# Gated hidden values made transposed, with gates spread over rows by way of DRAM

## The chip, the cores and the metric

One core of a Trainium2 chip. The metric is the device time of one execution in microseconds. In the profile PE is TensorE, DVE is VectorE, ACT is ScalarE, POOL is GpSimd, and SP is the engine that issues most DMAs.

## What is computed

Spatially reduced attention, and then a mixture of eight rank-16 adapters of which each token uses two. In the reference's terms, cut to what matters (B = 4, C = 128, 12288 queries and 768 keys for each b, N = 49152 tokens in all, E = 8, r = 16):

```python
kv_pool = kv.reshape(B, H // 4, 4, W // 4, 4, C).mean(axis=(2, 4))
k = v = kv_pool.reshape(B, -1, C) @ w_sr
a = softmax(q @ k.T / sqrt(C))
x = (a @ v).reshape(N, C)
logits = x @ w_gate                      # (N, 8)
top2 = the two largest logits;  w = softmax over these two
out = x + sum over e in top2 of w[e] * ((x @ A[e]) @ B[e])
```

With all A side by side (128 x 128, columns (e, r)) and all B stacked (rows (e, r)), the last line is `x + ((x @ A) * gate) @ B`, where a token's gate of e stands for 16 columns and is zero for six of the eight experts. Of two logits the softmax is (1 + tanh(d / 2)) / 2; the half is put into B.

## The kernel before

The tokens are worked in 96 chunks of 512 (24 for each b), each of four subtiles of 128. A chunk passes through these steps; each helper writes instructions in the order in which its engine will run them, since the schedule is by hand and every engine runs its own list in order.

- `scores(c, r)`, three times a chunk: two 512-column matmuls (L284) of two key tiles with the chunk's transposed queries `qT` into `sg` (two buffers of two PSUM banks), and one exponential of 1024 columns on ACT (L285) into `tt`.
- `weigh(c, h)`, twice a chunk: 12 matmuls of 137 columns (L297), weights `tt`, moving `vext` (values, values times gate matrix, ones), into `xps`.
- `normalise(c)`: on DVE a reciprocal (L304), the product `xn` (L308; output values and logits) and four MAX8 (L315).
- `gate(p)` and `gate_weights(p)` for a pair p of chunks: small operations on POOL (L324 to L327, L334, L335) with a tanh on ACT (L332) between; result `gw`, tokens in rows.
- `transposed(cx, ch)`: PE transposes the upper half of `xn` of chunk cx and the gated hidden `hg` of chunk ch, four matmuls of 128 columns each (L352), into one bank `t_ps`; its `evacuate` copies both to `xh` in one DVE operation (L361).
- `down(c)`: four matmuls with x transposed as weights and A moving (L375), into `h_ps`, tokens in rows; `apply_gate(c)`: DVE multiplies by the gates (L380) into `hg`.
- `up(c)`: four matmuls with hg transposed as weights and B moving (L400), into `d_ps`; `give(c)`: DVE adds `xn` (L407) into `osb`, and SP stores 256 KB (L413).

In iteration c of the main loop (c = 2 to 94) PE's list is: scores; the first half of weigh(c-1); scores; up(c-6); the second half of weigh(c-1); transposed(c-2, c-4); scores; down(c-3). `h_ps` and `d_ps` share one PSUM bank (`mtile`), `t_ps` is one bank, `xps` two, `sg` four: all eight. In odd iterations `gate_weights` of the pair c-3, c-2 is issued after the first scores.

Queries: `cast_q(g)` (POOL's DMA) writes 2048 rows as float16 to DRAM, `load_q(g)` (L274, SP) transposes all 2048 by one DMA into one of three buffers. Keys and values of the next b are loaded by SP (L85, 512 KB each, the last issued in iteration 55), summed on POOL and projected in the loop's `prep_step`. The first two query groups are `q0`, in a buffer of the kv pool, and `q1`, in one of its own.

After the loop come the run-out (weighing of chunks 94 and 95, and the steps of the last chunks, written out singly) and a range check that decides about a slow exact path, which isn't taken here.

Of the kernel before, what the change touches and what calls it, by code (L numbers as in the profile page):

```python
# [21 lines left out]
def kernel(  # L22
# [36 lines left out]
    ps_x = ctx.enter_context(tc.tile_pool(name="ps_x", bufs=1, space=bass.MemoryType.PSUM))  # L59
    ps_t = ctx.enter_context(tc.tile_pool(name="ps_t", bufs=1, space=bass.MemoryType.PSUM))  # L60
    ps_h = ctx.enter_context(tc.tile_pool(name="ps_h", bufs=1, space=bass.MemoryType.PSUM))
    score_banks = ExitStack()
# [8 lines left out]
    q_h = qdram.tile([B * N, C], F16)  # L71
    qflat = q.rearrange("b n c -> (b n) c")
# [8 lines left out]
    def load_row(b, t, d):  # L81
        if d == 0:
            kvt[b, t] = kvpool.tile([P, 4, 2, 4 * C], FP32, tag="kvt", name="kvt")
        src = kv[b].rearrange("(t h d) (w e) c -> t d h w (e c)", t=NT, d=4, e=8)
        nc.sync.dma_start(kvt[b, t][:, d].rearrange("p u c -> p (u c)"), src[t, d])  # L85
# [11 lines left out]
    q1 = kvpool.tile([P, GROWS // NTOK, NS, C], FP32, tag="q1", name="q1", bufs=1)  # L97
    q0 = kvpool.tile([P, GROWS // NTOK, NS, C], FP32, tag="kvt", name="q0")
# [37 lines left out]

    rinv_all = keep.tile([P, NCH, NS], FP32, name="rinv_all")
    vss = keep.tile([P, 2 * B], FP32, name="vss")
    kpT, kfT, vext, sqsum = {}, {}, {}, {}
    for b in range(B):  # L140
        kpT[b] = keep.tile([P, NKV], FP32, name=f"kpT{b}")
# [130 lines left out]
    def load_q(g):  # L272
        qT[g] = qpool.tile([P, GROWS], F16, tag="qT", name="qT")
        nc.sync.dma_start(qT[g], q_h[g * GROWS:(g + 1) * GROWS], transpose=True)  # L274
# [55 lines left out]
    def gate_weights(p, eng):  # L330
        th = small.tile([P, 2 * NS, E], FP32, tag="th", name="th")
        nc.scalar.activation(th, garg[p], AF.Tanh, bias=0.0, scale=0.5)  # L332
        gw[p] = small.tile([P, 2 * NS, E], FP32, tag="gw", name="gw")
# [3 lines left out]
    def transposed(cx, ch, bank=None):  # L337

        if bank is None:
            t_ps = ps_t.tile([P, 2, NS, P], BF16, tag="tp", name="t_ps")  # L340
        else:
            t_ps = bank.bitcast(BF16).rearrange("p (k s c) -> p k s c", k=2, s=NS)
# [6 lines left out]
        if not todo:  # L349
            return lambda act=False: None  # L350
        for i, (k, s, src) in enumerate(todo):
            mm(t_ps[:, k, s], src, id_bf, is_transpose=True,  # L352
               start=(i == 0), stop=(i == len(todo) - 1), skip_group_check=True)

        def evacuate(act=False):
            xh = run.tile([P, 2, NS, P], BF16, tag="xh", name="xh", bufs=5)
            lo, hi_ = todo[0][0], todo[-1][0] + 1
            if act:
                nc.scalar.activation(xh[:, lo:hi_], t_ps[:, lo:hi_], AF.Copy)  # L359
            else:  # L360
                nc.vector.tensor_copy(xh[:, lo:hi_], t_ps[:, lo:hi_])  # L361
            if lo == 0:
                xT[cx] = xh[:, 0]
            if hi_ == 2:
                hgT[ch] = xh[:, 1]

        return evacuate
# [35 lines left out]
    def give(c, how="add", queue=None):  # L403

        osb = run.tile([P, NS, P], FP32, tag="osb", name="osb", bufs=8)
        if how == "add":
            nc.vector.tensor_tensor(osb, dps[c], xn[c][:, :, 0:C], op=ALU.add)  # L407
        else:
            nc.scalar.activation(osb, dps[c], AF.Copy)
        if how == "pool":  # L410
            nc.gpsimd.tensor_tensor(osb, osb, xn[c][:, :, 0:C], op=ALU.add)  # L411
        t0 = c * NTOK
        (queue or nc.sync).dma_start(  # L413
            out[t0:t0 + NTOK, :].rearrange("(p s) c -> p s c", p=P), osb)

    def chunk_ok(c):
        return 0 <= c < NCH
# [121 lines left out]
    load_q(2)  # L539
# [10 lines left out]
    NQ = NCH // GRP  # L550
    for c in range(2, NCH - 1):
        b, k = divmod(c, CPB)
        cs = c + 2
        if cs < NCH and cs % GRP == 0:
            g = cs // GRP
            if g + 2 < NQ:
                load_q(g + 2)
            if g + 3 < NQ:
                cast_q(g + 3)
# [231 lines left out]
```

## Time and profile before

| | us |
|---|---|
| median of 3 runs (394.89 to 395.4) | 394.91 |
| the profiled execution | 395.21 |
| its span, first to last instruction | 393.4 |
| PE / DVE / ACT / POOL busy | 377.9 / 323.4 / 305.9 / 206.9 |
| mean granted TensorE clock | 0.997 |

A row of a timeline has start, duration, engine, line, operation, tiles and shapes, the number of merged instructions, and in brackets the idle time before it with what ended it. A row of a group has busy time and the mean ns of one behind the bar, then the idle time before. "To landing" is from a DMA's issue to its completion. Matmuls overlap, so a matmul's duration is longer than the distance to the next one's start.

### The profile page before, as it was taken

How to read it: one execution, taken by the hardware profiler on the slowest of the kernel's cores; microseconds unless marked ns; L12 is line 12 of the kernel's file. 1: busy time of each engine (PE TensorE's matmuls, PEld its weight loads, DVE VectorE, ACT ScalarE, POOL GpSimd, SP SyncE). 2: the span in 40 equal slices, each digit the busy share in tenths (PEclk: the TensorE clock that was granted, in tenths of full speed). 3: DMA queues.
4: the chain of work that ended last, by engine and by line, in shares of the span. 5: the costliest groups of instructions: out<-in, count | busy, mean ns of one | idle time of the engine just before them, and what ended most of it. 6: DMA issues, size and time to landing. Idle time of an engine off the chain costs nothing.

```text
span 393.4 us, 11525 instructions
## 1 busy us (share of the span) xinstructions
PE 377.9 (96%) x4589; PEld 301.2 (77%) x4589; DVE 323.4 (82%) x911; ACT 305.9 (78%) x387; POOL 206.9 (53%) x389
## 2 busy tenths in 40 slices
PE   4989999999999999999999999999999999999993
PEld 1457768888887887888878888888788888878882
DVE  3776777888888889888888888888888888888984
ACT  1558888878888888887877888888878877877863
POOL 1011598895688666563487666573442332322353
PEclk9999999999999999999999999999999999999998
DMA  8989997998898899298997998275678583222124
GB/s 255 393 279 167 358 262 229 275 218 218 258 211 234 256 164 266 83 211 246 238 238 225 241 237 211 92 166 130 135 92 205 136 188 102 88 82 83 55 86 160
DMA packets 69784, 76.47 MB, mean 194 GB/s; under 512 B 49664, under 2 KB 49920, under 8 KB 69376
## 3 DMA queue, kind: packets, MB, share of 16 engines
q1 hardware_dynamic: 67264, 63.45, 55.8%
q0 software_dynamic: 704, 11.54, 16.9%
q10 hardware_dynamic: 1760, 0.73, 0.7%
q8 instruction: 36, 0.59, 0.6%
q14 instruction: 20, 0.16, 0.1%
HBM read 50.53 MB, written 36.70 MB: 222 GB/s over the span
## 4 chain that ended last, share of the span: by engine, by line
PE 93%; ACT 2%; DMA 1%; POOL 1%; DVE 1%; issue 0%; ACTq 0%; POOLq 0%
PE xps L297 34%; PE sg L284 31%; PE t_ps L352 11%; PE d_ps L400 5%; PE h_ps L375 5%; PE w_ps L495 2%; PE v_ps L173 1%; DMA w_gate_sb<-in_moe_w_gate_dram 1%; ACT tt L285 1%; PE k_ps L198 1%; PE kp_ps L165 1%; ACT qT L481 0%; PE t_ps L477 0%; ACT xh L359 0%; POOL osb L411 0%
## 5 line engine op out<-in xcount | busy, mean ns | idle before, releaser
L285 ACT ACTIVATE tt<-sg 128x1024 f16<-128x1024 f32 x288 | 281.3, 1024 | 57.2 <-PE sg L284 56.8
L284 PE MATMUL sg<-qT,kfT 128*128 128x512 f16 x576 | 171.0, 379 | 1.3 <-ACT tt L285 1.0
L297 PEld LDWEIGHTS <-tt 128*128 128x128 f16 x2304 | 152.6, 112 | 22.1 <-DVE xn L308 0.7
L297 PE MATMUL xps<-vext,tt 128*128 128x137 f16 x2304 | 169.4, 223 | 0.0
L407 DVE TENSOR_TENSOR osb<-d_ps,xn 128x512 f32<-128x512 f32 x90 | 62.3, 692 | 35.3 <-PE d_ps L400 35.2
L324 POOL TENSOR_TENSOR arg<-xn,top 128x64 f32<-128x64 f32 x47 | 14.9, 317 | 121.6 <-DVE top L315 116.5
L308 DVE TENSOR_TENSOR xn<-xps,rinv_all 128x548 f32<-128x548 f32 x96 | 70.0, 729 | 3.3
L380 DVE TENSOR_TENSOR hg<-h_ps,gw 128x512 bf16<-128x512 f32 x93 | 63.2, 679 | 2.4 <-PE h_ps L375 2.4
L149 POOL TENSOR_TENSOR kvt<-kvt 128x1024 f32<-128x1024 f32 x27 | 63.9, 2368 | 1.3 <-PE sg L284 1.1
L361 DVE COPY xh<-t_ps 128x1024 bf16<-128x1024 bf16 (+1 forms) x93 | 62.5, 672 | 0.0
L284 PEld LDWEIGHTS <-kfT 128*128 128x128 f16 x576 | 45.0, 98 | 3.6 <-issue 2.1
L375 PEld LDWEIGHTS <-xh 128*128 128x128 bf16 x384 | 29.3, 98 | 21.5
L400 PEld LDWEIGHTS <-xh 128*128 128x128 bf16 x384 | 29.1, 98 | 21.5 <-ACT xh L359 0.6
L315 DVE MAX8 top<-xn 128x8 f32<-128x8 f32 x384 | 35.9, 156 | 3.3
L352 PE MATMUL t_ps<-id_bf,hg 128*128 128x128 bf16 x376 | 36.3, 219 | 0.5 <-ACT xh L359 0.5
L352 PE MATMUL t_ps<-id_bf,xn 128*128 128x128 bf16 x376 | 36.3, 219 | 0.0
L400 PE MATMUL d_ps<-b_bf,xh 128*128 128x128 bf16 x368 | 35.6, 219 | 0.5 <-ACT xh L359 0.5
L375 PE MATMUL h_ps<-a_bf,xh 128*128 128x128 bf16 x372 | 35.9, 219 | 0.0
L352 PEld LDWEIGHTS <-xn 128*128 128x128 bf16 x384 | 26.4, 98 | 0.7 <-DVE xn L308 0.4
L352 PEld LDWEIGHTS <-hg 128*128 128x128 bf16 x384 | 25.3, 98 | 0.9 <-DVE hg L380 0.8
L334 POOL TENSOR_SCALAR th<-th 128x64 f32<-128x64 f32 x48 | 18.0, 375 | 13.7 <-ACT th L332 13.5
L304 DVE RECIPROCAL rinv_all<-xps 128x4 f32<-128x4 f32 x96 | 17.5, 183 | 7.5 <-PE xps L297 5.0
(112 smaller groups left out, 240.2 us busy)
## 6 DMA issues: line engine op xcount, KB each, us to landing
kvt<-in_kv_dram SPq DMA_DIRECT2D x48, 512.0 KB, 6.1
out_dram<-osb SPq DMA_DIRECT2D x94, 256.0 KB, 3.0
q_h<-in_q_dram POOLq DMA_DIRECT2D x22, 512.0 KB, 7.1
q<-in_q_dram SPq DMA_DIRECT2D x2, 1024.0 KB, 9.9
out_dram<-osb ACTq DMA_DIRECT2D x2, 256.0 KB, 3.5
qT<-q_h SPq DMA_TRANSPOSE x22, 8.4
w_in<-in_w_sr_dram ACTq DMA_DIRECT2D x1, 64.0 KB, 1.8
a_f<-in_moe_A_dram ACTq DMA_DIRECT2D x1, 64.0 KB, 10.5
```

Of the source, the lines that this page charges most:

```text
L149: eng.tensor_tensor(v[:, 0], v[:, 0], v[:, d], op=ALU.add)
L284: mm(sg[:, k], kfT[b][:, j * P:(j + 1) * P], qc, start=True, stop=True)
L285: nc.scalar.activation(tt[c][:, 2 * r:2 * r + 2], sg, AF.Exp, bias=0.0, scale=scale)
L297: mm(o, tt[c][:, j, rows], vext[b][:, j, 0:VW], start=(j == 0 and s % 2 == 0), stop=(j == NJ - 1 and s % 2 == 1), skip_group_check=True)
L308: nc.vector.tensor_tensor(xn[c].rearrange("p (b s) v -> p b s v", b=2), xv, ri.rearrange("p (b s) -> p b s", b=2).unsqueeze(3).broadcast_t ...
L315: nc.vector.max(gin[c // 2][:, (c % 2) * NS + s], xn[c][:, s, C:C + E])
L352: mm(t_ps[:, k, s], src, id_bf, is_transpose=True, start=(i == 0), stop=(i == len(todo) - 1), skip_group_check=True)
L361: nc.vector.tensor_copy(xh[:, lo:hi_], t_ps[:, lo:hi_])
L375: mm(hps[c][:, s], xT[c][:, s], a_bf, start=(s == 0), stop=(s == NS - 1))
L380: nc.vector.tensor_tensor(hg[c].rearrange("p s (e r) -> p (s e) r", r=RK), hps[c].rearrange("p s (e r) -> p (s e) r", r=RK), g.rearrange(" ...
L400: mm(dps[c][:, s], hgT[c][:, s], b_bf, start=(s == 0 and fresh), stop=(s == NS - 1), skip_group_check=True)
L407: nc.vector.tensor_tensor(osb, dps[c], xn[c][:, :, 0:C], op=ALU.add)
```

## The change

For chunks 28 to 89 (`FAR`) the hidden values are made with rows (e, r) and tokens in columns: A is the weight and x transposed moves, one matmul of 512 columns. What `up` needs comes out of the multiplication directly, and hg is not transposed. The gates must then lie in the same layout, each in 16 rows: PE transposes the gates of a pair of chunks (128 columns, into the free part of `t_ps`), DVE copies 64 rows of it to `g_sb`, SP stores these to DRAM (`g_h`, 16 KB), and SP loads them back with each row repeated 16 times (`ge`, 256 KB a pair).

```diff
+    def load_gates(p):
+        gE[p] = run.tile([P, 2 * NS, P], F16, tag="ge", name="ge", bufs=3)
+        nc.sync.dma_start(
+            gE[p].rearrange("p s t -> p (s t)"),
+            g_h[p].rearrange("e s t -> e (s t)").unsqueeze(1).broadcast_to([E, RK, 2 * NS * P]))
+
+    def gated_hidden(c):
+        h_ps = mtile([P, NS, P], name="h_ps")
+        mm(h_ps, a_bf, xT[c], start=True, stop=True)
+        hgT[c] = run.tile([P, NS, P], BF16, tag="ht", name="ht", bufs=3)
+        nc.vector.tensor_tensor(hgT[c], h_ps, gE[c // 2][:, (c % 2) * NS:(c % 2 + 1) * NS],
+                                op=ALU.mult)
...
+        def later():                         # in transposed(cx, ch, p)
+            if p < NCH:
+                k = p % 4 // 2 * 2
+                mm(t_ps[:, 1, 0].bitcast(F16),
+                   gw_all[:, k:k + 2].rearrange("p k s e -> p (k s e)"), id_h,
+                   is_transpose=True, start=False, stop=True, skip_group_check=True)
...
+            if p < NCH:                      # in its evacuate
+                g_sb = small.tile([P, P], F16, tag="gt", name="g_sb", bufs=2)
+                copy(g_sb[rows], t_ps[rows, 1, 0].bitcast(F16))
+                nc.sync.dma_start(g_h[p].rearrange("e s t -> s e t"), g_sb[rows])
...
+    FAR = range(28, NCH - 6)
+    for x in FAR[::2]:
+        late = x == FAR[0]
+        sent[x + 3 + late] = x // 2
+        fetched[x + 4 + late] = x // 2
+    for x in range(NCH - 6):
+        far = x in FAR
+        made.setdefault(x + (6 if far else 3), []).append(x)
+        ups.setdefault(x + (7 if far else 6), []).append(x)
+        if not far:
+            turns[x + 4] = x
     for c in range(2, NCH - 1):
...
-        if chunk_ok(c - 6):
-            up(c - 6)
-            give(c - 6)
+        for x in ups.get(c, ()):
+            up(x)
+            give(x)
+        if c in fetched:
+            load_gates(fetched[c])
         weigh(c - 1, 1)
...
-        evacuate = transposed(c - 2, c - 4)
+        later, evacuate = transposed(
+            c - 2, turns.get(c, c - 4 if c == NCH - 2 else NCH),
+            sent.get(c, NCH))
         next_scores()
+        g, i = divmod(c + 2 * GRP, GRP)
+        if g < NQ:
+            load_q(g, i)
         prep(c)
...
-        if chunk_ok(c - 3):
-            down(c - 3)
-            apply_gate(c - 3)
+        for x in made.get(c, ()):
+            if x in FAR:
+                gated_hidden(x)
+            else:
+                down(x)
+                apply_gate(x)
+        later()
...
         evacuate(c == NCH - 2)
```

So a far chunk x (x even) has its pair's gates transposed in iteration x+3, fetched in x+4, and is multiplied in x+6 and x+7; `up` comes one iteration later than before. For other chunks the order is as before.

Besides: `load_q(g, k)` transposes 512 rows at a time, for chunk c+8 in iteration c. q0 and q1 share one kv buffer. The last kv tile is loaded in halves. The pooled keys stand in one tile. `osb` has six buffers instead of eight. The store of osb is split from its making (`take`, `add`, `add_rows`, `put`).

The run-out has a new order. The gates of chunks 94 and 95 are made chunk by chunk (94 on POOL, 95 on DVE), with MAX8 into the same places; chunk 95's weighing has banks of its own. Its list, with the loop's last steps, is in short:

```python
weigh(94, 0); gated_hidden(89); up(88); give(88); weigh(94, 1); tops4(94)
transposed(93, 91) -> ACT; up(89); h2 = hidden(92); up(90); gate_args(94) on POOL
weigh(95, 0); gated(92); turn x of 94; h3 = hidden(93); gated(93); weigh(95, 1)
up(91); tanh of 94; gate_w(94) on POOL; tops4(95); turn hg of 92; hidden(94); turn hg of 93
x_first(93); turn x of 95; gate_args(95), tanh of 95; up(92); gated(94); up(93); gate_w(95)
hidden(95); gated(95); POOL adds x of 89 to 92 to what ACT copied from d; puts
turn hg of 94; turn hg of 95 in two halves (ACT, DVE); up(94); give(94)
up(95) in two halves: ACT copies one (x added by PE), DVE adds x to the other; put(95)
```

`turn` is four transposes and a copy (ACT), `hidden` is `down` without the gate, `gated` is the multiplication of `apply_gate`.

299 lines of the change are left out of this document (204 added, 95 removed).

## The prediction

> **What bounds the kernel now.** I read the page first: the busy shares, then the chain that ended last.
>
> ```profile
> PE 377.9 (96%) x4589; PEld 301.2 (77%) x4589; DVE 323.4 (82%) x911; ACT 305.9 (78%) x387; POOL 206.9 (53%) x389
> ```
>
> ```profile
> PE 93%; ACT 2%; DMA 1%; POOL 1%; DVE 1%; issue 0%; ACTq 0%; POOLq 0%
> ```
>
> TensorE (PE) is busy 96% of the span, and 93% of the chain is its own work. A busy PE is not proof, so I went on to the timeline of one steady iteration, PE's rows and then VectorE's (DVE's): the starts of successive groups give the rate.
>
> ```profile
> 202.18 0.59 PE L284 MATMUL sg<-qT,kfT 128*128 128x512 f16 x2
> 202.61 0.39 PE L400 MATMUL d_ps<-b_bf,xh 128*128 128x128 bf16 x4
> 202.83 0.88 PE L297 MATMUL xps<-vext,tt 128*128 128x137 f16 x12
> 203.55 0.39 PE L352 MATMUL t_ps<-id_bf,xn 128*128 128x128 bf16 x4
> 203.77 0.39 PE L352 MATMUL t_ps<-id_bf,hg 128*128 128x128 bf16 x4
> 204.00 0.59 PE L284 MATMUL sg<-qT,kfT 128*128 128x512 f16 x2
> 204.43 0.39 PE L375 MATMUL h_ps<-a_bf,xh 128*128 128x128 bf16 x4
> 204.65 0.59 PE L284 MATMUL sg<-qT,kfT 128*128 128x512 f16 x2
> 205.08 0.88 PE L297 MATMUL xps<-vext,tt 128*128 128x137 f16 x12
> 205.80 0.59 PE L284 MATMUL sg<-qT,kfT 128*128 128x512 f16 x2
> 206.24 0.39 PE L400 MATMUL d_ps<-b_bf,xh 128*128 128x128 bf16 x4
> ```
>
> ```profile
> 203.03 0.69 DVE L407 TENSOR_TENSOR osb<-d_ps,xn 128x512 f32<-128x512 f32 x1 [0.37 <-PE d_ps L400]
> 203.75 0.18 DVE L304 RECIPROCAL rinv_all<-xps 128x4 f32<-128x4 f32 x1
> 203.97 0.73 DVE L308 TENSOR_TENSOR xn<-xps,rinv_all 128x548 f32<-128x548 f32 x1
> 204.73 0.37 DVE L315 MAX8 top<-xn 128x8 f32<-128x8 f32 x4
> 205.03 0.67 DVE L380 TENSOR_TENSOR hg<-h_ps,gw 128x512 bf16<-128x512 f32 x1
> 205.61 0.68 DVE L361 COPY xh<-t_ps 128x1024 bf16<-128x1024 bf16 x1
> ```
>
> From d_ps to the next d_ps is 206.24 - 202.61 = 3.63 us, the time of a chunk. No PE row has an idle note, and the starts follow at the length of the work: two 512-column score matmuls 0.43 (204.00 to 204.43), four 128-column ones 0.22 (203.55 to 203.77). So PE sets the loop by throughput, and work taken from PE comes off the time one for one until the next engine or chain is reached.
>
> **PE in the loop.** For 62 chunks (28 to 89) the change takes away four transposes of hg (L352) and four matmuls of h (L375), and puts in one 512-column matmul of h, plus one 128-column transpose of gates per pair of chunks. Removed: 248 transposes at 0.45/8 = 0.056 us (203.55 to 204.00 for eight) is 13.9, and 248 h matmuls at 0.22/4 = 0.055 is 13.6. Added: 62 x 0.43/2 = 13.3, and 31 x 0.056 = 1.7. The net is 12.5 us, or 0.20 a chunk: 3.63 becomes 3.43. Everything else on PE keeps its count.
>
> **DVE.** It keeps osb, reciprocal, xn, the maxima and one gating multiply of 512 elements; I take the multiply at its present 0.67, as only its second operand changes. The copy of xh halves, and once per pair a copy of 64 rows of 128 gates comes in.
>
> ```profile
> L361 DVE COPY xh<-t_ps 128x1024 bf16<-128x1024 bf16 x90 | 61.3, 681 | 0.0
> ```
>
> ```profile
> L361 DVE COPY xh<-t_ps 128x512 bf16<-128x512 bf16 x3 | 1.2, 415 | 0.0
> ```
>
> So 0.27 goes; the gate copy, by the slope of these two rows (0.266 per 512 elements), is 0.415 - 0.2 = 0.22, on alternate chunks. DVE now works from 203.03 to 206.29, 3.26 us of 3.63. It will need 3.0 and 3.2 of 3.43. Two of its chains run back into PE. First, d_ps to the gating multiply's end is 205.70 - 202.61 = 3.09, and the next d_ps (same bank) starts a period later: 0.54 to spare now, 0.34 after. Second, xn ends at 204.70 and the next weighing overwrites its bank at 205.08: 0.38 now. PE has 0.22 less between weighing and weighing (the hg transposes), and the h matmul is as long as the four were, so 0.16 is left, 0.05 more where a gate transpose stands. Both still fit, the second narrowly.
>
> **ScalarE (ACT).**
>
> ```profile
> 202.83 0.26 ACT L332 ACTIVATE th<-arg 128x64 f32<-128x64 f32 x1
> 202.97 1.03 ACT L285 ACTIVATE tt<-sg 128x1024 f16<-128x1024 f32 x1
> 204.63 2.89 ACT L285 ACTIVATE tt<-sg 128x1024 f16<-128x1024 f32 x3 [0.63 <-PE sg L284]
> ```
>
> Three exponentials start (2.89 - 1.02)/2 = 0.93 apart when they run together, so 2.8 a chunk plus half a tanh (0.26/2). Far from 3.43. The distance from the third scores of a chunk to the second of the next, within which an exponential must free the bank, is unchanged, since h takes as long as before.
>
> **The gates' way.**
>
> ```profile
> 203.63 0.32 POOL L335 TENSOR_TENSOR gw<-th,msk 128x64 f32<-128x64 f32 x1
> ```
>
> The gates are done on POOL at 203.95 in their iteration; PE transposes them after h, at about 204.4 on the shortened scale, so PE does not wait while POOL is on time; its long kv sums stand behind these weights in program order. DVE's copy follows the multiply and ends at about 205.95 on this scale; SP then stores 16 KB. One iteration on, SP waits for the store to land and issues a 256 KB load that repeats each row 16 times; the gating multiply needs it three iterations after 205.03, at 205.03 + 3 x 3.43 = 215.3. So store, wait and load together have 215.3 - 206.0 = 9.3 us. Chunk 28 alone is sent an iteration late and has 5.9. What do transfers take? The nearest rows are the puts of osb, 256 KB each, first for 160 to 185 us (kv loads running), then for 250 to 300 (none left):
>
> ```profile
> DMA to landing us min/median/max: 2.0/4.1/8.6
> ```
>
> ```profile
> DMA to landing us min/median/max: 2.0/2.2/8.2
> ```
>
> The two trips are 2 x 4.1 = 8.2 in the first case, and 2 x 2.2 = 4.4 in the second; the ends are 2 x 2.0 = 4.0 and 2 x 8.6 = 17.2. I take the medians: hidden in both, by 1.1 and by 4.9. Behind SP's wait stand the next query transpose, used six iterations later, and the next put, whose osb is ready about a period later; nobody waits for either. The osb buffers fall from eight to six, some 20 us, against puts that land in 8.6 at most: zero.
>
> **Is there room in the DMA engines?**
>
> ```profile
> 190.00:210.00 20.00, 20.00 (x254) 16.08 (x253) 17.48 (x52) 16.41 (x19) 12.27 (x22) 1.00 0.98 264
> 310.00:330.00 20.00, 20.00 (x259) 16.30 (x257) 17.62 (x51) 16.44 (x20) 6.45 (x19) 1.00 0.49 121
> 350.00:370.00 20.00, 20.00 (x258) 16.26 (x256) 18.24 (x52) 16.35 (x20) 5.41 (x16) 1.00 0.18 68
> ```
>
> ```profile
> kvt<-in_kv_dram SPq DMA_DIRECT2D x48, 512.0 KB, 6.1
> out_dram<-osb SPq DMA_DIRECT2D x94, 256.0 KB, 3.0
> ```
>
> In the three windows the last columns are DMA share and GB/s. At 350 to 370 there are only puts: 0.18 x 20 / (20/3.63) = 0.65 us of all engines each. A gate load moves as much to SBUF, so it adds some 0.65 per 6.9 us, a tenth of the engines. That is nothing at 310, and it fills the engines at 190 to 210, where the share is 0.98 already; the kv loads end with chunk 55, so 10 of the 31 pairs are stored beside them. The Trainium skill ("DMA: Bandwidth & Descriptors", the sections on why a DMA increments its semaphore by 16 and Rules for kernel authors) speaks against the load's shape: a pattern whose slowest dimension is 8, as here, runs on 8 of the 16 engines, so these would carry twice that share; by it I estimate a fifth instead of a tenth on half the engines, and up to 4 us of the gain gone in the kv stretch, so 387 for 383. No row of before shows a load of that shape. It raises the chance of the first rival below and not the sum.
>
> **Queries by chunk.** Each 512 KB transpose becomes four, at the same bytes, each issued six iterations ahead. The wait of SP for a free qT falls away, as the buffer asked for has been read out by then:
>
> ```profile
> SPq L274 <- PE sg L284: 38.7, 9, 6.6
> ```
>
> SP's idle time is worth nothing itself; I take zero. A quarter transpose has six iterations, 6 x 3.43 = 20.6 us, to land. The smaller edits (q0 and q1 in one kv buffer, one tile for the pooled keys, the last kv tile in halves) touch loads that lie iterations ahead: zero, covered by that lead; if the second kv batch came late behind q1 it would cost at most about one load, 6 us, which is inside the first rival's price.
>
> **The run-out.** Rows of its two ends, and of two kinds of step in it:
>
> ```profile
> 379.84 1.60 PE L297 MATMUL xps<-vext,tt 128*128 128x137 f16 x24
> ```
>
> ```profile
> 387.79 0.69 DVE L407 TENSOR_TENSOR osb<-d_ps,xn 128x512 f32<-128x512 f32 x1 [0.17 <-PE d_ps L400]
> ```
>
> ```profile
> L409 ACT ACTIVATE osb<-d_ps 128x512 f32<-128x512 f32 x2 | 1.2, 597 | 0.6 <-PE d_ps L400 0.6
> ```
>
> ```profile
> L324 DVE TENSOR_TENSOR arg<-xn,top 128x64 f32<-128x64 f32 x1 | 0.2, 236 | 0.0
> ```
>
> Weighing ends at 381.44, the last DVE operation at 388.48: 7.0 us, then 4.9 to the span's end at 393.4 (the span as the page gives it) for the last put. In the new order the last chunk goes reciprocal, xn, maxima (1.3), gate arguments (four like L324, 0.9), tanh, weight, multiply (0.26 + 0.24 + 0.67 = 1.2), a half transpose, a half copy (0.3), up, and an add of 256 (0.4): with some 0.2 for each of four hand-overs (the 0.37 ahead of osb holds one) about 5 us of dependent steps if each engine is free. But ACT has five earlier copies of 0.6 (L409 above) queued from about 381.4 on ahead of that tanh, so I place tanh's end 3.4 after the weighing, not 2.5, and two more copies of 0.6 ahead of the last chunk's; the last add then ends at about 6.7. That gains 0.3; the bounds are 2.0 (only the dependent steps) and -1.5 (two and a half more copies in the way). After 381.44 the old order has 56 matmuls of 128 columns in bfloat16, the new one 48; so 8 x 0.056 = 0.4 of the 12.5 lies where PE waits for others, and is not gained.
>
> **Sum.** The profiled execution took 395.21 us, 1.8 beside its span of 393.4. 395.2 - 12.5 + 0.4 - 0.3 = 382.8. The median of the runs is 394.91, 0.3 less, within what runs differ by; I say 383. About 0.2%, 0.8 us, is what a measurement can tell.
>
> **Rivals.**
>
> *The gate loads come late beside the kv loads.* For it: share 0.98, puts up to 8.6, so a pair can need more than 9.3. Against it: quarter transposes leave shorter queues ahead of a store. If the ten pairs lose 0.4 to 1.0 us each, 4 to 10 are lost: 387 to 393. The rule on 8 engines above is one way into this case.
>
> *Slower than before: the round trip sets the pace.* Where store and load take L, three chunks pass in L + 1.0 (206.0 - 205.03) or more, so the chunk takes (L + 1.0)/3: at L = 9.9 this is 3.63 and the whole gain is gone, at L = 10.5 it is 3.83 and 62 x 0.2 = 12 us are lost against before, 407. It decides when the mean trip exceeds 9.9. For it: SP holds all transfers behind its wait, and two medians in the loaded stretch already make 8.2. Against it: after 250 us they make 4.4, so this must hold in a stretch with free engines too.
>
> *DVE takes over.* If xn, at 0.16 to spare, holds the weighing by another 0.1 a chunk, 62 x 0.1 = 6 are lost: 389. For it: the margin; against it: DVE itself has 0.2 idle per chunk.
>
> *PE does not speed up.* If the one 512-column h matmul exposes its weight load and drain, or PE waits for the gates' transpose, 0.2 a chunk is given back: no change, 395. The score matmuls of the same width run at 0.215 with nothing exposed, which speaks against it.
>
> **Numbers.** Forecast as summed, 380 to 387: 0.62. First rival, 387 to 393: 0.18. DVE, 387 to 391: 0.07. No change: 0.03. Slower: 0.10. The range 380 to 392 leaves out the last two, a little of the first rival, and a better run-out below 380. Faster: 0.62 + 0.18 + 0.07 = 0.87.
>
> **What would show it.** Right: a d_ps-to-d_ps period near 3.43 from chunk 34 on, no idle note ahead of PE rows in the loop; the multiply on the gate tile never waits for a DMA; the last weighing ends about 12 us earlier, and the last DVE operation some 6.7 after it. Wrong: a wait list led by the multiply for its gate load, or by the weighing for xn; a period that differs between the kv stretch and after; SP waits for gate stores of 5 us and more.

## The result and the profile after

The changed kernel is slower: 439.18 us (median of 4 runs, 436.22 to 445.06) against 395.15 of the kernel before in the same session, a ratio of 1.108 (95% interval 1.100 to 1.116). 383 was predicted, with a range up to 392. Medians and ranges are of all runs; some executions of any kernel here fall into a state that makes them some per cent longer, and the ratios leave these out, so that e13, with one run left, has none, and e14's and e18's are lower than their medians would give. The profiled execution took 436.22 us, its span is 434.4, the mean granted clock 0.96.

The page of the changed kernel, busy shares and chain:

```profile
PE 379.4 (87%) x4190; PEld 286.2 (66%) x4190; DVE 316.6 (73%) x943; ACT 308.8 (71%) x391; POOL 206.2 (47%) x393
```

```profile
PE 59%; DMA 28%; DVE 7%; ACT 2%; SPq 2%; issue 1%; POOL 0%; DVEq 0%; ACTq 0%
```

PE was on 93% of the chain and is on 59%; DMA had 1% and has 28%, some 120 us. Which DMA, and who waits for it, the list of waits says (total, times, longest):

```profile
PEld L443 <- DVE ht L409: 48.7, 23, 10.5
DVE ht L409 <- DMA ge<-g_h: 44.5, 16, 10.5
PE d_ps L443 <- DVE ht L409: 37.9, 14, 10.0
...
PEld L310 <- DVE xn L321: 10.0, 45, 0.4
```

The gating multiply (L409) waits for the load of the gates 16 times, and `up` (L443) waits for the multiply: the first of the signs of being wrong that the prediction named. The last row is the narrow chain from `xn` to the weighing: often late, never by more than 0.4 us.

The second sign, a period that differs between the kv stretch and after, came too (table below); the third, SP waiting 5 us and more for a gate store, did not. SP's own list of waits from 149 to 273 us, while the kv loads run, is led by

```profile
SPq L400 <- DMA g_h<-g_sb: 25.3, 11, 3.2
```

that is 25.3 us in 11 waits, none over 3.2; over the whole run it is 44.4.

Where no load is waited for, the loop is as forecast. PE's and DVE's timelines of the changed kernel:

```profile
205.80 0.39 PE L443 MATMUL d_ps<-b_bf,ht 128*128 128x128 bf16 x4
...
207.40 0.38 PE L407 MATMUL h_ps<-xh,a_bf 128*128 128x512 bf16 x1
207.61 0.22 PE L369 MATMUL t_ps<-id_h,gw_all 128*128 128x128 f16 x1
...
209.25 0.39 PE L443 MATMUL d_ps<-b_bf,ht 128*128 128x128 bf16 x4
```

```profile
188.79 0.23 DVE L378 COPY g_sb<-t_ps 64x128 f16<-64x128 f16 x1
...
204.82 0.67 DVE L409 TENSOR_TENSOR ht<-h_ps,ge 128x512 bf16<-128x512 f32 x1
205.41 0.41 DVE L378 COPY xh<-t_ps 128x512 bf16<-128x512 bf16 x1
```

From d_ps to d_ps is 3.45 us. Now the path of one pair's gates. The chain in order of time (start, us, what), and SP's own list over the same stretch:

```profile
174.80 4.00 DMA g_h<-g_sb
...
178.87 5.88 DMA ge<-g_h
...
187.29 5.45 DMA g_h<-g_sb
...
192.76 3.56 DMA ge<-g_h
```

```profile
187.29 0.62 SPq L383 DMA_DIRECT2D g_h<-g_sb  x1
187.95 3.15 SPq L462 DMA_DIRECT2D out_dram<-osb  x1
192.76 0.60 SPq L400 DMA_DIRECT2D ge<-g_h  x1
193.47 1.15 SPq L287 DMA_TRANSPOSE qT<-q_h  x1
194.72 0.52 SPq L462 DMA_DIRECT2D out_dram<-osb  x1
195.29 1.16 SPq L287 DMA_TRANSPOSE qT<-q_h  x1
196.50 0.59 SPq L93 DMA_DIRECT2D kvt<-in_kv_dram  x1
197.19 0.62 SPq L383 DMA_DIRECT2D g_h<-g_sb  x1
```

Two delays add up. Store and load take 9.9 and 9.0 us, not 8.2. And the store starts late: the copy that ended at 189.02 is stored at 197.19, because SP was held 3.15 us in the issue of a put, then waited 1.7 at the load for the store before it (under way for 5.45 in all), and then had 4.4 us of issuing to do, two transposes of 1.15 among it. SP goes round in 9.9 us for two chunks, which should take 6.9. From 149 to 273 us its issues add up to 87.5 us and its waits for gate stores to 25.3, of 124: the list is nearly full.

Over the 14 pairs of chunks 28 to 55 the medians are 5.6 us from the copy's end to the issue of its store (longest 15.8), 3.7 from there to the issue of the load, and 5.8 from there to the multiply where that waited. Over the 17 pairs of chunks 56 to 89 they are 1.8, 2.0 and 5.3. From the copy's end to the first multiply by its gates a pair takes 15.1 us on average in the first group and 10.8 in the second; 9.3 was foreseen.

Where each kernel loses is read from the start of the reciprocal of a chunk in DVE's timeline. The table has the time from one chunk's to another's, for these two kernels and five of the experiments:

| chunks (us) | before | changed | e1 | e11 | e16 | e17 | e18 |
|---|---|---|---|---|---|---|---|
| 28 to 56 | 104.8 | 136.8 | 100.0 | 110.2 | 104.8 | 104.8 | 104.8 |
| 56 to 90 | 125.1 | 130.7 | 118.9 | 121.3 | 124.5 | 125.1 | 119.5 |
| 93 to the end | 16.8 | 19.6 | 19.5 | 23.7 | 19.5 | 18.9 | 18.3 |

Against e1, in which store and load are left out, the changed kernel loses 36.8 us in chunks 28 to 56, beside the kv loads, and 11.8 in chunks 56 to 90.

### The profile page after: what moved, and what is told of

The parts are those of the page before. It is cut to its first block, busy times and chain, and to the rows that moved or that the text cites. A ratio compares the mean times of both kernels' runs of the same rounds, so it can differ in the third digit from the quotient of the medians.

```text
span 434.4 us, 11005 instructions
## 1 busy us (share of the span) xinstructions
PE 379.4 (87%) x4190; PEld 286.2 (66%) x4190; DVE 316.6 (73%) x943; ACT 308.8 (71%) x391; POOL 206.2 (47%) x393
## 4 chain that ended last, share of the span: by engine, by line
PE 59%; DMA 28%; DVE 7%; ACT 2%; SPq 2%; issue 1%; POOL 0%; DVEq 0%; ACTq 0%
PE xps L310 23%; PE sg L297 19%; DMA ge<-g_h 16%; DMA g_h<-g_sb 10%; PE t_ps L361 5%; PE d_ps L443 4%; DVE ht L409 2%; DMA kvt<-in_kv_dram 2%; PE h_ps L407 2%; PE h_ps L418 1%; DVE xn L321 1%; ACT tt L298 1%; PE v_ps L183 1%; PE w_ps L547 1%; SPq L287 1%
## 5 line engine op out<-in xcount | busy, mean ns | idle before, releaser
L297 PE MATMUL sg<-qT,kfT 128*128 128x512 f16 x576 | 173.8, 385 | 1.4 <-ACT tt L298 1.0
L310 PEld LDWEIGHTS <-tt 128*128 128x128 f16 x2304 | 155.5, 113 | 23.8 <-DVE xn L321 10.0
L409 DVE TENSOR_TENSOR ht<-h_ps,ge 128x512 bf16<-128x512 f32 x62 | 42.2, 680 | 45.6 <-DMA ge<-g_h 44.5
L443 PE MATMUL d_ps<-b_bf,ht 128*128 128x128 bf16 x240 | 24.3, 226 | 38.2 <-DVE ht L409 37.9
L443 PEld LDWEIGHTS <-ht 128*128 128x128 bf16 x248 | 17.6, 100 | 58.1 <-DVE ht L409 48.7
L378 DVE COPY xh<-t_ps 128x512 bf16<-128x512 bf16 (+1 forms) x92 | 45.6, 495 | 0.5
L407 PE MATMUL h_ps<-xh,a_bf 128*128 128x512 bf16 x62 | 24.5, 395 | 0.1
L423 DVE TENSOR_TENSOR hg<-h_ps,gw_all 128x512 bf16<-128x512 f32 x30 | 20.4, 680 | 1.0 <-PE h_ps L418 1.0
L340 POOL TENSOR_SCALAR msk<-msk 128x64 f32<-128x64 f32 x47 | 17.4, 371 | 4.2
L348 POOL TENSOR_TENSOR gw_all<-th,msk 128x64 f16<-128x64 f32 x47 | 15.1, 321 | 3.9
```

The costliest lines, as they stand in the source:

```text
L297: mm(sg[:, k], kfT[b][:, j * P:(j + 1) * P], qc, start=True, stop=True)
L310: mm(o, tt[c][:, j, rows], vext[b][:, j, 0:VW], start=(j == 0 and s % 2 == 0), stop=(j == NJ - 1 and s % 2 == 1), skip_group_check=True)
L378: nc.vector.tensor_copy(dst, src)
L407: mm(h_ps, a_bf, xT[c], start=True, stop=True)
L409: nc.vector.tensor_tensor(hgT[c], h_ps, gE[c // 2][:, (c % 2) * NS:(c % 2 + 1) * NS], op=ALU.mult)
L443: mm(dps[c][:, s], hgT[c][:, s], b_bf, start=(s == 0 and fresh), stop=(s == NS - 1), skip_group_check=True)
```

## The experiments

Ratios are to the kernel before, run beside each, with their 95% intervals. Four theories were open at first: SP's wait for the store (A), the transfers' own length (B), the run-out (C), and later the casts of the queries (D).

**e1: no trip.** Store and load are left out, far chunks are multiplied by ones.

```diff
-                nc.sync.dma_start(g_h[p].rearrange("e s t -> s e t"), g_sb[rows])
...
+        gE[p] = ge_one
```

> Neither the store nor the load of the gates: far chunks are multiplied by a constant tile of ones instead of their gates. All else as in the changed kernel, the gates' transpose and its copy included. Both theories of the trip (A: SP's wait in its list; B: the transfers themselves are too slow) give the time that the prediction had worked out, 383 (381 to 386), with some 3.45 us a chunk. A third, that the new loop or the run-out is slow by itself, gives over 395.

387.76 us, 0.978 (0.973 to 0.984). So the trips cost 51 us, and everything else in the change together brings 8, not 12.

**e2: no wait.** The load reads a block filled once at the start, so SP waits for no store; the gates are ones.

```diff
-            g_h[p].rearrange("e s t -> e (s t)")...
+            g_fix.rearrange("e s t -> e (s t)")...
```

> The store and the load of the gates stay at their places and sizes, but the load reads another piece of DRAM that was filled once at the start (ones instead of gates), so that SP's load waits for no store. A (SP waits some 3.6 to 5.5 us a pair for the store to land, with everything else queued behind it): most of the loss goes, 383 to 392. B (the load's own way, 3.6 to 7.4 us with half the engines, in crowded queues): it stays above 415.

407.65 us, 1.025 (1.018 to 1.033). Here SP's wait is worth some 32 of the 51; 20 are left although nothing is waited for before the load. In this kernel's waits:

```profile
DVE ht L413 <- DMA ge<-g_fix: 17.1, 7, 4.7
```

**e3: later load**, at the head of the next iteration. **e4: whole queries**, 2048 rows per transpose as before.

```diff
-        fetched[x + 4 + late] = x // 2
+        fetched[x + 5] = x // 2
```

```diff
-        nc.sync.dma_start(qT[g][:, k * NTOK:(k + 1) * NTOK], q_h[r:r + NTOK], transpose=True)
+        nc.sync.dma_start(qT[g], q_h[g * GROWS:(g + 1) * GROWS], transpose=True)
```

> The load of a pair's gates is issued at the head of iteration x+5 instead of within x+4, nothing left out. The store has then landed or nearly so (some 2.5 us more after its issue), and the load has about 5.7 us to its first use at 3.43 us a chunk. A: SP's list keeps up, 385 to 395, with short waits where a load takes over 5.7. B: the load has less time than before, so no better than 430.

> The queries are transposed 2048 rows at a time by one DMA, at the iterations of the kernel before; the gates' way is that of the change. A: SP's list per pair of chunks is shorter by about one issue of 1.15 us, but single transposes hold it longer: 420 to 440. If the quartered transposes (88 issues of 1.15 us or more) were the cause by themselves, it would come back to 385 to 395. B: 435 to 445.

e3: 425.15 us, 1.069 (1.060 to 1.077); neither theory's number. e4: 419.5 us, 1.051 (1.041 to 1.060): the quartering takes 20 us in this kernel.

**e5: store from ScalarE.**

```diff
-                nc.sync.dma_start(g_h[p]...
+                nc.scalar.dma_start(g_h[p]...
```

> One edit to the changed kernel: the store of the turned gates is issued from ScalarE's queue instead of SyncE's. Nothing is left out. Theory A (the gates wait in SyncE's list: the store is issued some 8 us after its copy is done, because SyncE still stands at the wait for the store before): the store goes out as soon as the copy is made and has landed when SyncE comes to the load, so SyncE waits for it rarely and the time falls to about that of the kernel without the wait, 405 to 412 us. Theory B (the way itself is too long wherever the store is issued): 428 to 440 us. ScalarE pays some 0.6 us of issue per pair, at most 3 us in all if it has no room.

422.18 us, 1.066 (1.062 to 1.070). The store goes out 0.03 us after the copy (median), but A's number is missed, for the wait moved to ACT, which stands at the store until DVE has copied, and PE's scores wait for ACT. Chunks 28 to 56 take 118.1 us for 136.8, but 56 to 90 take 134.4 for 130.7. In its waits:

```profile
PE sg L297 <- ACT tt L298: 15.1, 26, 4.4
...
ACT tt L298 <- DVE xh L378: 14.4, 12, 1.5
...
DVE ht L409 <- DMA ge<-g_h: 8.1, 5, 4.4
```

**e6: sixteen engines.** e2 with the row order turned, so that the load's outermost dimension is 16.

```diff
-g_fix.rearrange("e s t -> e (s t)").unsqueeze(1).broadcast_to([E, RK, 2 * NS * P])
+g_fix.rearrange("e s t -> e (s t)").unsqueeze(0).broadcast_to([RK, E, 2 * NS * P])
```

> The kernel whose load takes its rows from a block that is filled once at the start (so SyncE waits for no store; the gates are ones), 407.6 us, with one edit: the rows of the load are walked in the other order, sixteen repeats on the outside and eight experts inside, so that the outermost dimension is 16 long instead of 8. Theory of the eight engines (a load with an outermost dimension of 8 goes by half of the engines and takes twice as long): the load's way falls by 1 to 2 us and the time to 395 to 402 us. Theory of the casts (packets of 32 KB hold the load on every engine it uses): 404 to 411 us, or more, since more engines have to be free.

404.9 us (401.32 to 411.93), 1.025 (1.020 to 1.029): no difference to e2 beyond the scatter. The trace has 8 more 4-byte packets per load, one for each engine added, so the load was spread; that is not what it lacked.

**e7 and e9: few casts.** The casts from the eighth group on are left out (5 of 22 stay), and the queries from the seventh group on are read from the sixth group's rows; e7 on top of e2, e9 on top of the changed kernel.

```diff
-        if cs < NCH and cs % GRP == 0 and cs // GRP + 3 < NQ:
+        if cs < 4 * GRP and cs % GRP == 0:
...
-        r = g * GROWS + k * NTOK
+        r = min(g, 5) * GROWS + k * NTOK
```

> The kernel whose load takes its rows from a block that is filled once at the start (so SyncE waits for no store; the gates are ones), 407.6 us, with one edit: the casts of the queries from the seventh group on are left out (17 or 18 of them), and the queries of these groups are read from the rows of the sixth. Theory of the casts (their packets hold the gates' load for some 6 us, once in four chunks): the time falls to 390 to 398 us. Theory of the eight engines, or of SyncE's issue time: 403 to 408 us, since neither is touched.

> The changed kernel with one edit: the casts of the queries from the seventh group on are left out, and the queries of these groups are read from the rows of the sixth. Stores, loads and SyncE's wait for the store stay. Theory D (the casts' packets hold every transfer that meets them, the gates' store and load among them, and SyncE's wait only passes that on): the trips shorten to some 6 us and the time falls to 389 to 400 us. Theory A (SyncE's list and its wait are enough by themselves): 415 to 425 us, that is 20 us less than the changed kernel, as between the two kernels without the wait.

e7: 389.07 us, 0.985 (0.982 to 0.987). e9: 400.09 us, 1.012 (1.008 to 1.016). With e2 and the changed kernel that makes four corners: 439 with both, 408 without the wait, 400 without the casts, 389 without either, and 388 without the trip. The two causes make each other worse: alone the wait costs 11 us and the casts cost 19, together they cost 50. Theory D's number is met at its edge. Without the casts SP's issues get shorter too: those of the 88 transposes last 122 us in e9 and 157 in the changed kernel. The casts' share of the engines stands in the DMA part of the pages; of before, e1 and e7:

```profile
q1 hardware_dynamic: 67264, 63.45, 55.8%
q0 software_dynamic: 704, 11.54, 16.9%
```

```profile
q1 hardware_dynamic: 70240, 63.98, 62.2%
q0 software_dynamic: 704, 11.54, 18.0%
```

```profile
q1 hardware_dynamic: 76688, 72.62, 72.6%
q0 software_dynamic: 160, 2.62, 3.7%
```

(Queue, packets, MB, time of the packets as a share of 16 engines' span.) A cast takes 16.9% of 393.4 us / 22 = 3.0 us of all 16 engines. The trips add (72.6% of 386.7 - 62.2% of 385.2) / 31 = 1.3 us a pair. The rest of the change, e1 against before, adds 62.2% of 385.2 - 55.8% of 393.4 = 20 us; in it the 4-byte packets go from 2.6 to 19.7 us of all engines, as 88 transposes took the place of 22 (e4, with 22, has 2.5). These sums of packet times are not a fixed price: by e15 (below) against e1, with all casts in both, the same trips come to (75.6% of 393.8 - 62.2% of 385.2) / 31 = 1.9 us a pair.

**e8: only chunks 84 to 89**, queries whole (e4's edit): the new run-out nearly alone.

```diff
-    FAR = range(28, NCH - 6)
+    FAR = range(84, NCH - 6)
```

> The changed kernel with two edits: only chunks 84 to 89 go the new way, and the queries are turned by whole groups, as in the kernel before. Nothing is left out. What remains of the change is its new run-out, and three trips of the gates. Theory C (the new run-out costs 2.7 us, as its stretch from the last normalising in the loop to the end was 19.3 to 19.4 us in two kernels against 16.55 us before): 396.5 to 400 us against 395.2 to 395.7 before. Its rival (the new run-out is worth its 0.3 us, and the longer stretch is what the trips leave behind, or comes from a lower clock): 393.5 to 395.5 us.

398.14 us, 1.008 (1.006 to 1.010): theory C's number, 3 us.

**e10: casts in quarters**, one a chunk. **e11**: the same, with the store from ScalarE behind the next chunk's first scores, so that ACT needn't wait, and the load at the head of the next chunk but one.

```diff
+        if cs >= GRP and cs // GRP + 3 < NQ:
+            cast_q(cs // GRP + 3, cs % GRP)
...
+                pend.append(lambda: nc.scalar.dma_start(g_h[p]...
...
+        while pend:
+            pend.pop()()
+        if c in fetched:
+            load_gates(fetched[c])
```

> The changed kernel with one edit: from the fifth group on, each cast of 2048 query rows becomes four casts of 512 rows, one in each chunk, with the same lead before the rows are read. The bytes are the same, each packet is a quarter (8 KB); nothing is left out. If the length of the casts' packets is what holds the gates' transfers: within 6 us of the kernel with few casts that is run beside it. If the bytes of the casts are what counts: within 8 us of the changed kernel, 430 to 440 us.

> The changed kernel with three edits, and nothing left out: casts in quarters, one a chunk; the store of the turned gates from ScalarE's queue, behind the first scores of the next chunk so that ScalarE doesn't wait for the copy; the load at the head of the next chunk but one. If SyncE's list, the casts' packets and nothing else made the trips late: no wait of the gated product for the load, and the time of the kernel without trips, 386 to 391 us, below the kernel before (395). If the bytes of the casts count, not their packets: 400 to 410 us.

e10: 429.52 us, 1.086 (1.080 to 1.092): just under the number for bytes (430 to 440) and far from the one for packets (within 6 us of e9's 400), so the packets' length is not the main point. It is not nothing either: in the traces chunks 30 to 90 take 247.4 us against 259.7 in the changed kernel (225.7 in e9), while e10's end is 4.3 us longer for another reason, told at the bottom. e11: 408.79 us, 1.031 (1.026 to 1.036), the number for bytes. In chunks 56 to 90 e11 is faster than before (table); it loses 5.4 us beside the kv loads and 6.9 at its end, some 4 of these for the same other reason. **e12**, e11 with GpSimd making the last chunk's gate arguments:

```diff
-    gate_args(n, 0, NS, nc.vector, top5, arg5, msk5)
+    gate_args(n, 0, NS, nc.gpsimd, top5, arg5, msk5)
...
+    add(n - 6, o6, nc.gpsimd)
+    put(n - 6, o6)
     gate_w(0, NS, nc.gpsimd, arg4, msk4)
```

> The kernel with the three edits (casts in quarters, store from ScalarE, later load) with a changed run-out beside them: the last chunk's gate arguments are made on GpSimd instead of VectorE, one of GpSimd's four sums of outputs is moved ahead of them and the other three come after. Nothing is left out. If the new run-out's 3 us come from VectorE's two small sums of 1.1 to 1.2 us each beside GpSimd's sums: 1 to 2 us less than that kernel, and no small operation of the run-out over 0.4 us on either engine. If they come from the order of the work elsewhere: within 0.5 us of that kernel.

407.13 us, 1.024 (1.020 to 1.029), not told apart from e11 by time. In the traces the stretch from chunk 93 to the end is 1.7 us shorter (22.05 for 23.71), the first reading's number, and the last sum ends 6.9 us after the last reciprocal begins against 7.6. But one small operation is still over 0.4 us, beside POOL's sums:

```profile
394.83 0.91 DVE L709 SCALAR_TENSOR_TENSOR r<-r,r 128x32 f32<-128x32 f32 x1 [0.94 <-ACT r L704]
```

**e13: whole queries (e4's edit) with e11's store and load, whole casts**, and e12's run-out but with the fourth sum on VectorE. **e14**: the same for chunks 56 to 89 only, `FAR = range(56, NCH - 6)`.

```diff
-    o2 = take(n - 3)
...
+    give(n - 3)
-    for c, o in ((n - 6, o6), (n - 5, o0), (n - 4, o1), (n - 3, o2)):
+    for c, o in ((n - 5, o0), (n - 4, o1)):
```

> The changed kernel with the queries turned by whole groups as before, whole casts as before, the store of the turned gates from ScalarE's queue behind the next chunk's first scores, the load at the head of the next chunk but one, and a run-out in which GpSimd makes the last chunk's gate arguments ahead of all but one of its sums. Nothing is left out. Theory E (the DMA engines have no time left between chunks 28 and 78, so that what counts is the sum of their packets' time; the quarter transposes put some 24 us of all engines into 4-byte semaphore writes, 26.4 against 2.6 before): those 24 us come back and the time is 394 to 403 us, against 409 of the kernel with quarters and the same store and load. Theory F (the engines have time; what counts is where a gate transfer stands in its queue): 404 to 412 us, since whole transposes of 512 KB stand ahead of the loads.

> The same kernel with only chunks 56 to 89 done the new way, so that no gate trip lies beside a kv load. Nothing is left out. Theory E: after the kv loads the engines are 0.57 to 0.71 busy in the kernel before, the loads have room, and 34 chunks gain 0.18 us each, 6 us; with a run-out as long as the old one the time is 388 to 391 us, faster than the kernel before. Theory F: some 10 of the 17 pairs still meet a cast or a transpose, and the time is 394 us or more.

e13: 416.05 us (407.02 to 418.88), every run over E's 394 to 403. e14: 404.69 us (398.75 to 409.98), 1.011 (1.007 to 1.014): F's number. It lost nearly 5 us at one place, where a store of 16 KB took 9.61 us in the chain:

```profile
288.56 9.61 DMA g_h<-g_sb
298.24 4.10 DMA ge<-g_h
```

Just ahead of it SP had issued a whole transpose and POOL a whole cast, which landed at 297.94:

```profile
287.61 3.43 SPq L284 DMA_TRANSPOSE qT<-q_h  x1
...
287.85 0.59 POOL L103 DMA_DIRECT2D q_h<-in_q_dram  x1
```

The DMA share from 242 to 284 us, before this place, is 0.73, so here the burst just ahead held it rather than a lasting lack of engine time.

**e15: the same traffic, nobody waits.** e2's load goes to a tile that isn't read; ones are multiplied.

```diff
-        gE[p] = run.tile([P, 2 * NS, P], F16, tag="ge", name="ge", bufs=3)
+        gE[p] = ge_all
+        unread = run.tile([P, 2 * NS, P], F16, tag="ge", name="ge", bufs=3)
```

> The kernel whose load takes its rows from a block that is filled once at the start (407.6 us), with one edit: the loads go to a tile that nobody reads, and the far chunks are multiplied by a tile of ones that is there from the start. The DMA traffic is the same, but nobody waits for it. Theory E, in its strong form (the engines have so little time that queries, kv rows or outputs come late too): 398 to 408 us. In its weak form (what lies six iterations ahead still comes in time; only the gates, with two chunks of lead, are late): 387 to 391 us, the time of the kernel without the trip.

397.06 us, 1.002 (1.000 to 1.005). Of the 9 us to e1, 2.7 lie before chunk 5, and 5.5 in chunks 52 to 56, where the gate stores (5.36 and 5.43 us in its chain) held DVE's copy into `g_sb` by its two buffers. From chunk 60 to 90 it takes 104.5 us, as e1 does. So the queries, kv rows and outputs still come in time, though the engines are full; only the gates, with under three chunks of lead, are late. The windows (last columns DMA share and GB/s; a share may pass 1, as packets overlap) of the kernel before and then of e15:

```profile
256.00:315.00 59.00, 59.00 (x750) 47.88 (x747) 50.85 (x145) 48.44 (x61) 25.58 (x60) 1.00 0.66 144
```

```profile
196.00:224.00 28.00, 27.97 (x321) 21.01 (x319) 23.76 (x77) 24.25 (x30) 21.35 (x35) 1.00 1.22 263
...
259.00:315.00 56.00, 55.99 (x644) 42.68 (x642) 48.16 (x152) 48.77 (x61) 25.19 (x61) 1.00 0.98 201
```

**e16: chunks 56 to 89**, with e11's store and load, queries by chunk, and from chunk 55 on each cast in two halves behind a gates' load. **e17**: the same with e13's run-out, its puts in the order in which they are ready.

```diff
+            m, half = divmod(c + 1, GRP)
+            if c > 54 and m + 3 < NQ:
+                cast_q(m + 3, half // 2, 2)
```

```diff
+    o2 = add_rows(n - 3)
+    put(n - 2, o3)
     for c, o in ((n - 5, o0), (n - 4, o1)):
         add(c, o, nc.gpsimd)
         put(c, o)
+    put(n - 3, o2)
```

> The changed kernel with four edits, nothing left out: only chunks 56 to 89 go the new way; the store of the turned gates is issued from ScalarE's queue behind the next chunk's first scores; the load at the head of the next chunk but one; and from chunk 55 on each cast is two halves, each issued behind a gates' load (14 casts for 7). Queries by chunk and run-out stay as in the changed kernel. Theory F (where a gate transfer stands among others in the queues decides; engine time is not short after the kv loads): no trip meets a whole cast or a whole transpose, the 34 chunks take 119 to 121 us against 125.1 before, the end costs 1.5 to 3 us more than before, and the time is 391 to 394 us, faster than the kernel before. Theory E (engine time is short as long as casts run): the chunks up to 80 lose as before, 395 to 400 us.

> The same kernel with the run-out changed beside: GpSimd makes the last chunk's gate arguments and sums one output ahead of them and two behind, VectorE sums the fourth, and the outputs are put in the order in which they are ready. Nothing is left out. If VectorE's two small sums of 1.1 to 1.2 us beside GpSimd's sums are what the end can do without: 0.5 to 1.5 us less than that kernel. If the end is set by the puts, which crowd behind the last chunk: the same within 0.4 us, or more.

e16: 397.55 us, 1.005 (1.002 to 1.008); e17: 396.25 us, 1.000 (0.997 to 1.003). Theory F's number, 391 to 394, is missed and E's, 395 to 400, is met: chunks 56 to 90 bring 0.6 us of the 6.2 that e1 has there, and the multiply waits 5.5 us for gate loads. e17's median is 1.3 us lower, and the two intervals overlap; in the traces its end is 0.6 us shorter.

**e18: early casts.** e17 with the last seven casts made in chunks 28 to 52, whole, and queries read before chunk 56 turned whole.

```diff
+        if 28 <= c < 56 and c % GRP == 0:
+            cast_q(17 + (c - 28) // GRP)
```

> The kernel with chunks 56 to 89 done the new way, store from ScalarE's queue, later load and the changed run-out, with the casts whole and the last seven (groups 17 to 23) made early, one each in chunks 28 to 52 beside the casts that are due there, so that no cast runs while gates travel; queries of the groups read before chunk 56 are turned whole, the later ones by chunk. Bytes are the same, nothing is left out. If the engines' time between chunks 56 and 80 is what the trips lack, and the kv stretch has some to spare: chunks 56 to 90 take 119 to 120 us against 125.1 before, the kv stretch loses 0 to 4, the end costs 1 to 2, and the time is 390 to 394 us, faster than the kernel before. If the kv stretch has none: it loses 5 us or more and the time is 395 us or more.

398.18 us, 1.005 (1.002 to 1.008). The mechanism came out and the time did not: chunks 56 to 90 take 119.5 us in the profile, 5.6 less than before, with no wait for a gate load, at a DMA share of 0.62 where e16 has 0.87. In e16's and e18's windows:

```profile
256.00:315.00 59.00, 56.02 (x632) 41.99 (x632) 46.68 (x149) 48.80 (x60) 27.87 (x65) 1.00 0.87 173
```

```profile
256.00:315.00 59.00, 58.63 (x673) 44.76 (x672) 48.37 (x157) 51.45 (x64) 24.77 (x62) 1.00 0.62 148
```

The kv stretch lost nothing (104.8 us). But 3.5 us more than before went between chunks 5 and 20, and 1.5 at the end. The 3.5 lie in one chunk: from the reciprocal of chunk 6 to that of chunk 7 it takes 7.12 us for 3.63. No chunk goes the new way there yet, and other executions lose time at the same place: e5, whose program up to chunk 28 is that of the changed kernel, takes 7.87 us there, and the changed kernel 3.63. So this loss need not belong to e18's edits; what it waits for is open. The profiled execution, 394.47 us, is the fastest of e18's. No version that leaves nothing out beat the kernel before.

## Why the prediction was wrong

- **PE in the loop**: right in kind. 3.43 was forecast, 3.45 stands in the timeline. Without trips (e1) chunks 30 to 90 take 211.1 us against 222.1, 0.18 a chunk for the 0.20 worked out.
- **DVE and ACT**: right. Copy of gates 0.23 for 0.22, multiply 0.67, halved copy 0.41; PE's scores wait 1.0 us for ACT in the whole run. The chain with 0.16 to spare is the one that shows (at most 0.4 us at a time).
- **The gates' way is the step that failed**, in three places. It let the store start when the copy ends; it starts 5.6 us later beside the kv loads and 1.8 after them. It said that behind SP's wait "nobody waits for either" the transpose or the put; but the next pair's store stands behind them in the same list, and everyone waits for that. And it took landing times from before (4.1 and 2.2): for the store they were about right (3.7 and 2.0), but where the multiply waited the load took 5.8 and 5.3.
- **Room in the DMA engines**: mis-sized by half. A pair was given 0.65 us of all engines and takes 1.3 (1.9 by e15); with the 20 us of the other edits the share of 0.66 from 256 to 315 becomes 0.98 (e15), and "nothing at 310" fell with it: from 310 to 330 e15 has 0.92, where 0.49 stood. Of the pairs 13, not 10, are stored up to iteration 55.
- **Queries by chunk, zero**: wrong. Four issues of 1.15 us or more on the engine whose list holds the gates (157 us in all, for 81 of the whole transposes before), and most of the 20 us of engine time. Undone alone, it gives 20 us back (e4). In other company it brought nothing that shows (e13, 407 us at best, against e11's 404 to 412); e14's store is one that stood behind a whole transpose.
- **The rule on 8 engines**, weighed at up to 4 us: what the Trainium skill says ("DMA: Bandwidth & Descriptors", the section on why a DMA increments its semaphore by 16) is borne out in the count of 4-byte packets, but e6 found no time in it.
- **The run-out**: -0.3 forecast, 2.8 more measured (19.6 against 16.8 in the table). 2.2 lie between the normalising of chunk 93 and that of chunk 95 (7.1 for 4.9): chunks 88 and 89 still want their last products there, which the step did not place, and DVE runs without a pause from one reciprocal to the next:

```profile
416.06 0.67 DVE L409 TENSOR_TENSOR ht<-h_ps,ge 128x512 bf16<-128x512 f32 x1
416.65 0.68 DVE L423 TENSOR_TENSOR hg<-h_ps,gw_all 128x512 bf16<-128x512 f32 x1
417.25 0.68 DVE L409 TENSOR_TENSOR ht<-h_ps,ge 128x512 bf16<-128x512 f32 x1
417.84 0.69 DVE L457 TENSOR_TENSOR osb<-e,xn 128x512 f32<-128x512 f32 x1
418.53 0.18 DVE L759 RECIPROCAL rinv_all<-y 128x4 f32<-128x4 f32 x1
```

  1.0 comes behind it: from the end of the weighing to the last sum it is 8.1 us, where 6.7 was forecast and 7.0 stood. What follows the last sum gives 0.4 back (4.5 for 4.9), but the end hangs on something else now: in the changed kernel it comes 0.8 us behind POOL's closing drain, which starts once the range check's flag is read, and before it came 3.4 us behind it, after the last put. The 1.0 has a place; POOL's and DVE's timelines of the changed kernel:

```profile
422.38 3.46 POOL L452 TENSOR_TENSOR osb<-osb,xn 128x512 f32<-128x512 f32 x3
```

```profile
423.53 1.22 DVE L696 TENSOR_TENSOR r<-xn,top 128x32 f32<-128x32 f32 x1
424.78 1.10 DVE L697 TENSOR_TENSOR r<-r,r 128x32 f32<-128x32 f32 x1
```

- **The rivals**: "the round trip sets the pace" is what came, at a chance of 0.10. Chunks 30 to 90 took 259.7 us, 4.33 a chunk, for which its formula wants L = 12.0; measured from the copy's end to the multiply, a pair takes 12.7 on average. Against it I had put that the engines are free after 250 us; the change itself fills them. But three quarters of the loss, 36.8 of 48.6 us against e1, lie beside the kv loads, the place of the first rival, which was given 4 to 10 us.

What stays open: whether a late store or load in e16 is held by the sum of the engines' time or by which transfer was queued just ahead. e18 (fewer transfers beside the trips, none waited for) fits both; e14's store speaks for the second, the numbers of e10, e11 and e16 for the first. Open too is how much of the loss goes with the lower clock (last point below).

## What to carry over

A small transfer on a path with a deadline must be budgeted by the list in which it is issued and by the engines' load after the change, not by landing times from before it; sum the packets' time of everything that the change adds, the splitting of transfers included. A wait put into an in-order DMA list delays every later issue in it, and the next round of the same trip is one of them. Where a trip can't be avoided, ask which other transfers can be moved out of its stretch: with the casts gone from it (e18) no gate load was waited for.

## What was not expected of the hardware

- DVE's small sums of two SBUF tiles took 1.22 and 1.10 us beside POOL's sums, and 0.21 and 0.25, twice as wide, in the kernel before. DVE's multiply with one operand in PSUM kept its 0.69 (at 426.90, beside the sum of 1.18 at 426.76). Made on POOL (e12, e17) the small sums take 0.25 each. The Trainium skill ("GPSIMD Engine Reference", Specifications) names this contention, for DVE instructions with two SBUF inputs; the rows agree.
- With 82 instead of 22 casts, POOL's closing drain lasted 6.76 us instead of 1.94 (five casts: 0.55), some 0.08 us a cast. That is most of e10's and e11's longer end.
- A transpose of 512 rows occupies SP for 1.13 us at least (median 1.17, up to 5.9), a gate store or load 0.6, a put 0.3.
- Where PE idles most for gates the granted clock (the last figure but two) is low; whether the idling is the cause was not tried. From 207 to 254 us of the changed kernel:

```profile
207.00:254.00 47.00, 30.59 (x318) 22.67 (x316) 24.52 (x76) 24.53 (x30) 24.43 (x37) 0.84 0.85 185
```

  Over chunks 28 to 56 it is 0.91, and 1.00 in e1; PE's busy time there is 107.7 us for 100.0, so up to 8 of the 36.8 us may go with the clock.
